# The last three tiles of a decode-attention kernel: a set order, loads in pieces, and the last V rows straight into the result

## Chip, cores, metric

One core of one Trainium2 chip in each set of runs. The metric is device microseconds of one execution. A profile gives, besides, the span from its first to its last instruction, here usually 1.7 to 2 us shorter than the device time.

## The reference, cut to what matters

```
B, H, Sq, Skv, Dh = 8, 32, 1, 4096, 128        # bf16
scores = einsum('bhqd,bhkd->bhqk', q, k) * Dh ** -0.5
attn   = softmax(scores)
out    = einsum('bhqk,bhkd->bhqd', attn, v)
```

There is one query row for each of 256 heads, so every byte of K and V (537 MB together) is used once.

## The kernel before

The heads go in NT = 64 tiles of four heads. K and V of a tile are 4 MB each; a partition holds C = 128 rows of 128 numbers. For each tile:

- `product`: VectorE multiplies K by the query in place (four pieces) and folds 128 columns to 64.
- `sum_over_d`: TensorE adds the 64 columns to 4 with 16 matmuls by the identity (tile `ps`).
- `weights_of`: VectorE adds those four, finds a maximum (`sc`, `pmax`, `spread`, `nmax`, `bias`); ScalarE does four exponentials (`w`).
- `values_of`: 32 matmuls of 512 columns (`av`), four V rows of each partition at a time.
- `result_of`: ScalarE copies `av` to `comb`; four small matmuls with `pick` add the wanted blocks into `op`; after four tiles ScalarE scales `op` by 1/sum and the result is stored.

The parts that the change touches:

```python
    v_cuts = {
        NT - 3: [C // 2] * 2,
        NT - 2: [C // 4] * 4,
        NT - 1: [C // 4] * 3 + [C // 8, C // 8],
    }
    # ... all loads go to one queue, nc.sync, into five 4 MB buffers
    for t in range(NT):
        if t + 2 < NT:
            load("k", t + 2)
        load("v", t)
        # ... q_prep
        product(t, 0, C // 2)
        if t > 0:
            weights_of(t - 1)
        product(t, C // 2, C)
        if t > 1:
            values_of(t - 2, 0, C)
            result_of(t - 2)
            # ... norm_of every fourth tile
        if t < NT - 1:
            sum_over_d(t)
    values_of(NT - 2, 0, C // 2)
    sum_over_d(NT - 1)
    values_of(NT - 2, C // 2, C)
    result_of(NT - 2)
    weights_of(NT - 1)
    norm_of(NQ - 1)
    values_of(NT - 1, 0, C)
    result_of(NT - 1)
```

A scheduler of the framework decides the order on each engine from this; it is not the order of the text. On every engine the instructions then run in that order, so one that waits holds up all behind it (the run with the pieces alone, below, shows two such waits of TensorE, 2.66 and 1.59 us).

## Time and profile before

| | before |
|---|---|
| device time, median of 3 | 1267.79 us (1266.04 to 1267.88) |
| profiled run: time, span | 1269.76, 1267.1 us |
| last V bytes arrive | about 1254 us of the span |
| from there to the end | 13 us |

The page's slices (40 equal ones, 31.7 us each): the busy share of the DMA engines in tenths, and what they moved.

```profile
DMA  9999999999999999999999999999999999999994
GB/s 399 430 430 430 431 432 435 429 431 435 431 430 431 431 430 431 430 433 431 429 430 431 431 434 431 432 429 432 433 432 432 430 431 430 429 429 430 433 425 197
```

Only the first slice and the last two are below the stream's rate. The Trainium skill ("DMA: Bandwidth & Descriptors", Specifications) gives 435 GB/s as the fabric's ceiling, and this trace agrees with 429 to 435 in the other 37. So the body of the kernel cannot go faster without moving fewer bytes. What is left is the end. Here is the chain of waits from 1190 us on: start, duration, and what the end waited for.

```profile
1188.82 36.04 DMA kt<-in_k_dram
...
1224.89 4.49 DVE kt L144 x2
...
1238.25 1.14 DVE kt L147
...
1239.56 1.74 ACT w L197 x8
...
1248.81 2.93 PE ps L161 x13
...
1253.67 1.73 ACT w L197 x8
...
1256.33 7.02 PE av L211 x32
```

The last K lands at 1224.9. Its product, mixed with the weights of tile NT-2, takes VectorE until 1239.4. The last sum (`ps`) is spread between values of NT-2 (the line shows its last 13 matmuls) and ends at 1251.7; only then can the last weights be made, and the last 32 value matmuls start at 1256.3, when all of V has been there for 2 us.

The stretches show what TensorE had to work with: length, busy us of each engine, granted TensorE clock, DMA share, GB/s.

```profile
core 0: us, PE busy (x) PEld busy (x) DVE busy (x) ACT busy (x) POOL busy (x), PEclk, DMA share, GB/s
1237.00:1241.00 4.00, 1.72 (x8) 0.46 (x5) 2.52 (x4) 1.44 (x7) 0.00 (x0) 0.95 1.02 424
1241.00:1245.00 4.00, 3.65 (x12) 1.06 (x12) 0.00 (x0) 0.72 (x3) 0.00 (x0) 0.50 1.01 421
1245.00:1249.00 4.00, 4.00 (x14) 1.01 (x13) 0.00 (x0) 0.00 (x0) 0.00 (x0) 0.70 0.84 345
```

TensorE is idle for more than half of the first stretch, and then gets half its clock for 6.8 us (1240.6 to 1247.4), just when the last sum should go through. The Trainium skill ("TensorE: Matmul & The Clock Gate", Part 1) says that a monitor sets the clock to full or half by windows of about 3.4 us that run freely, not in step with the kernel. The trace agrees: its clock records last 3.41 us or multiples of it and say 1.0 or 0.5.

### The profile page before, as it was taken

The numbers are of one execution on the slowest core, as the hardware profiler recorded it, in microseconds if no ns is written. First come the engines' busy times: TensorE is split into PE (matmuls) and PEld (weight loads), VectorE is DVE, ScalarE is ACT, GpSimd is POOL, SyncE is SP. The second block draws the span as 40 slices with busy tenths as digits, with TensorE's granted clock in tenths as the row PEclk, the third lists the DMA queues.
The fourth block names the chain that finished last, engine by engine and source line by source line (L and its number), as shares of the span: only waits on it lengthen the run. The fifth ranks groups of instructions, "written<-read, shape, count | busy, mean of one in ns | idle before, by whom it ended". The sixth has DMA issues, their size and how long they took to land.

```text
span 1267.1 us, 8759 instructions
## 1 busy us (share of the span) xinstructions
PE 848.8 (67%) x3424; PEld 316.9 (25%) x3424; DVE 939.4 (74%) x850; ACT 164.0 (13%) x609; POOL 2.7 (0%) x13
## 2 busy tenths in 40 slices
PE   1566776766856767658667676676676766757677
PEld 0222222222322222222222222222222222212222
DVE  5869978677687687776877867768678687786771
ACT  0101111111111111101011011110111101101111
POOL 0000000000000000000000000000000000000000
PEclk9778878888879788888787887888877878888888
DMA  9999999999999999999999999999999999999994
GB/s 399 430 430 430 431 432 435 429 431 435 431 430 431 431 430 431 430 433 431 429 430 431 431 434 431 432 429 432 433 432 432 430 431 430 429 429 430 433 425 197
DMA packets 19992, 537.55 MB, mean 424 GB/s; under 512 B 2528, under 2 KB 2528, under 8 KB 2800
## 3 DMA queue, kind: packets, MB, share of 16 engines
q1 hardware_dynamic: 19584, 536.88, 98.7%
q8 instruction: 26, 0.43, 0.1%
q10 hardware_dynamic: 368, 0.13, 0.0%
q14 instruction: 14, 0.11, 0.0%
HBM read 536.94 MB, written 0.07 MB: 424 GB/s over the span
## 4 chain that ended last, share of the span: by engine, by line
DMA 67%; PE 24%; DVE 7%; ACT 1%; issue 0%; DVEq 0%; ACTq 0%
DMA vt<-in_v_dram 63%; PE av L211 22%; DVE kt L144 4%; DMA kt<-in_k_dram 4%; DVE kt L147 2%; PE ps L161 2%; ACT w L197 1%; DVE sc L174 0%; PE op L236 0%; ACT comb L232 0%; DVE pmax L178 0%; DVE bias L189 0%; DVE spread L180 0%; DVE nmax L185 0%; PE zp L222 0%
## 5 line engine op out<-in xcount | busy, mean ns | idle before, releaser
L211 PE MATMUL av<-vt,w 128*16 128x512 bf16 x2048 | 574.8, 450 | 347.4 <-DMA vt<-in_v_dram 345.9
L144 DVE TENSOR_TENSOR kt<-kt,qb 128x4096 bf16<-128x4096 bf16 x256 | 579.3, 2284 | 218.8 <-DMA kt<-in_k_dram 218.7
L211 PEld LDWEIGHTS <-w 128*16 128x16 bf16 x2048 | 207.5, 102 | 711.0 <-issue 541.9
L147 DVE TENSOR_TENSOR kt<-kt 128x2048 bf16<-128x2048 bf16 x256 | 305.9, 1216 | 0.0
L161 PE MATMUL ps<-kt,ident 128*128 128x512 bf16 x1024 | 254.3, 391 | 33.4 <-DVE kt L147 33.4
L197 ACT ACTIVATE w<-sc,bias 128x128 bf16<-128x128 f32 x256 | 110.9, 567 | 749.5 <-DVE bias L189 749.5
L161 PEld LDWEIGHTS <-ident 128*128 128x128 bf16 x1024 | 90.8, 98 | 162.5 <-issue 63.2
L174 DVE TENSOR_REDUCE sc<-ps 128x128 f32<-128x512 f32 x64 | 43.8, 684 | 31.4 <-PE ps L161 31.4
L197 ACT ACTIVATION_READ_ACCUMULATOR w<-sc,bias 128x1 f32 x256 | 64.7, 253 | 0.0
L232 ACT ACTIVATE comb<-av 16x512 bf16<-16x512 f32 x64 | 37.6, 588 | 160.3 <-PE av L211 124.4
L227 DVE RECIPROCAL rz<-zp 16x1 f32<-16x1 f32 x16 | 2.5, 155 | 65.1 <-PE zp L222 65.1
L135 ACT ACTIVATE qb<-qp 128x512 bf16<-128x512 f32 x16 | 9.6, 597 | 178.9 <-DVE kt L144 173.7
L236 PE MATMUL op<-comb,pick 16*16 16x128 bf16 x256 | 25.2, 219 | 5.3 <-ACT comb L232 5.3
L236 PEld LDWEIGHTS <-pick 16*16 16x16 bf16 x256 | 13.8, 85 | 33.0 <-issue 33.0
L129 PE MATMUL qp<-q_all,ident 16*32 16x512 bf16 x64 | 7.6, 430 | 21.3 <-ACT qb L135 14.9
L178 DVE TENSOR_REDUCE pmax<-sc 128x1 f32<-128x128 f32 x64 | 17.8, 279 | 0.1
L180 DVE TENSOR_SCALAR spread<-zero,pmax 128x32 f32<-128x32 f32 x64 | 15.0, 235 | 0.1
L189 DVE TENSOR_SCALAR bias<-own,nmax 128x4 f32<-128x4 f32 x64 | 14.3, 224 | 0.1
L185 DVE TRANSPOSE_TENSOR_REDUCE nmax<-spread 128x1 f32<-128x32 f32 x64 | 13.1, 204 | 0.1
L129 PEld LDWEIGHTS <-ident 16*32 16x32 bf16 x64 | 1.8, 89 | 28.1 <-issue 26.5
L222 PE MATMUL zp<-ones,esum 128*16 128x1 f32 x32 | 3.1, 166 | 8.3 <-ACT w L197 8.3
L245 ACT ACTIVATE stage<-op,rz 16x128 bf16<-16x128 f32 x16 | 5.7, 357 | 10.7 <-PE op L236 10.7
(17 smaller groups left out, 7.6 us busy)
## 6 DMA issues: line engine op xcount, KB each, us to landing
kt<-in_k_dram SPq DMA_DIRECT2D x64, 4096.0 KB, 35.3
vt<-in_v_dram SPq DMA_DIRECT2D x61, 4096.0 KB, 29.6
vt<-in_v_dram SPq DMA_DIRECT2D x7, 1024.0 KB, 28.4
vt<-in_v_dram SPq DMA_DIRECT2D x2, 2048.0 KB, 27.3
vt<-in_v_dram SPq DMA_DIRECT2D x2, 512.0 KB, 17.9
q_all<-in_q_dram ACTq DMA_DIRECT2D x1, 64.0 KB, 5.6
out_dram<-stage ACTq DMA_DIRECT2D x3, 16.0 KB, 10.0
out_dram<-stage ACTq DMA_DIRECT2D x1, 12.0 KB, 8.7
```

The costliest lines, as they stand in the source:

```text
L144: nc.vector.tensor_tensor(out=part, in0=part, in1=qb[:, j : j + 1, :].to_broadcast([P, MC, D]), op=ALU.mult)
L147: nc.vector.tensor_tensor(out=part[:, :, 0 : D // 2], in0=part[:, :, 0 : D // 2], in1=part[:, :, D // 2 : D], op=ALU.add,)
L161: nc.tensor.matmul(ps[:], lhsT=ident[:], rhs=kt[:, u * UC : (u + 1) * UC, s * DS : (s + 1) * DS], start=(s == 0), stop=(s == n - 1),)
L174: nc.vector.tensor_reduce(out=sc[:, u * UC : (u + 1) * UC], in_=ps[:], axis=AX.X, op=ALU.add)
L178: nc.vector.tensor_reduce(out=pmax[:], in_=sc[:], axis=AX.X, op=ALU.max)
L180: nc.vector.tensor_scalar(out=spread[:], in0=zero[:], scalar1=pmax[:, 0:1], scalar2=-scale, op0=ALU.add, op1=ALU.mult,)
L185: nc.vector.tensor_reduce(out=nmax[:], in_=spread[:], axis=AX.X, op=ALU.min, apply_transpose=True)
L189: nc.vector.tensor_scalar(out=bias[:], in0=own[:], scalar1=nmax[:, 0:1], scalar2=None, op0=ALU.add)
L197: nc.scalar.activation(out=w[:, :, g], in_=sc[:], func=ACT.Exp, bias=bias[:, g : g + 1], scale=scale, accum_out=esum[:, t % R, g : g + 1],)
L211: nc.tensor.matmul(avs[t][:], lhsT=w[:, c0 : c0 + CB, :], rhs=vt[:, c0 : c0 + CB, :], start=(c0 == 0), stop=(c0 == C - CB),)
L232: nc.scalar.activation(out=comb[:], in_=avs.pop(t)[:], func=ACT.Copy)
L236: nc.tensor.matmul(ops[n][:], lhsT=pick[:, m, r, :], rhs=comb[:, m * D : (m + 1) * D], start=(r == 0 and m == 0), stop=(r == R - 1 and m = ...
```

## The change

Intent: bring the last product and the last sum forward by halving the last K load and by a hand-set order; cut the V loads finer; and take the last 8 of 128 V rows of each partition out of the block scheme, multiplying them by zero-padded weights straight into `op` (the "direct rows" below), so that they are needed only at the very end.

```diff
+LAST = 8
...
+    w_last = consts.tile([P, LAST, RG], BF16, name="w_last")
+    nc.gpsimd.memset(w_last[:], 0.0)
...
-    v_cuts = {
-        NT - 3: [C // 2] * 2,
-        NT - 2: [C // 4] * 4,
-        NT - 1: [C // 4] * 3 + [C // 8, C // 8],
+    cuts = {
+        ("k", NT - 1): [C // 2] * 2,
+        ("v", NT - 3): [C // 4] * 4,
+        ("v", NT - 2): [C // 4] * 4,
+        ("v", NT - 1): [C // 4] * 3 + [C // 8, C // 16, LAST],
     }
...                                   (in weights_of)
+        if t == NT - 1:
+            nc.vector.tensor_copy(out=w_last[:, :, RG - G : RG], in_=w[:, C - LAST : C, :])
...                                   (in result_of; the stop flags follow)
+        if t == NT - 1:
+            for i in range(LAST):
+                nc.tensor.matmul(
+                    ops[n][:], lhsT=w_last[:, i, :], rhs=loads["v", t][:, C - LAST + i, :],
+                    start=False, stop=(i == LAST - 1),
+                )
...
-    for t in range(NT):
+    for t in range(NT - 1):
...
-        if t < NT - 1:
-            sum_over_d(t)
-    (the end as shown above)
+        sum_over_d(t)
+    load("v", NT - 1)
+    with tc.manual_schedule():
+        product(NT - 1, 0, C // 2)
+        weights_of(NT - 2)
+        product(NT - 1, C // 2, C)
+        values_of(NT - 3, 0, C)
+        result_of(NT - 3)
+        sum_over_d(NT - 1)
+        values_of(NT - 2, 0, C // 2)
+        weights_of(NT - 1)
+        values_of(NT - 2, C // 2, C)
+        result_of(NT - 2)
+        norm_of(NQ - 1)
+        values_of(NT - 1, 0, C - LAST)
+        result_of(NT - 1)
```

More of the change, by code (lines that the diff above doesn't have):

```diff
@@ L116, in load @@
         c0 = 0
-        for n in v_cuts.get(t, [C]) if kind == "v" else [C]:
+        for n in cuts.get((kind, t), [C]):
             nc.sync.dma_start(buf[:, c0 : c0 + n, :], src[t, :, c0 : c0 + n, :])
@@ L212, in values_of @@
                 avs[t][:], lhsT=w[:, c0 : c0 + CB, :], rhs=vt[:, c0 : c0 + CB, :],
-                start=(c0 == 0), stop=(c0 == C - CB),
+                start=(c0 == 0), stop=(c0 + CB == (C if t < NT - 1 else C - LAST)),
             )
@@ L237, in result_of @@
                 ops[n][:], lhsT=pick[:, m, r, :], rhs=comb[:, m * D : (m + 1) * D],
-                start=(r == 0 and m == 0), stop=(r == R - 1 and m == CB - 1),
+                start=(r == 0 and m == 0), stop=(r == R - 1 and m == CB - 1 and t < NT - 1),
             )
+        if t == NT - 1:
[4 more added lines that the diff above has]
+                )
         if r < R - 1:
@@ L270 @@
                 norm_of((t - 2) // R)
-        if t < NT - 1:
-            sum_over_d(t)
-    values_of(NT - 2, 0, C // 2)
-    sum_over_d(NT - 1)
-    values_of(NT - 2, C // 2, C)
-    result_of(NT - 2)
-    weights_of(NT - 1)
-    norm_of(NQ - 1)
-    values_of(NT - 1, 0, C)
-    result_of(NT - 1)
+        sum_over_d(t)
[14 more added lines that the diff above has]
+        result_of(NT - 1)
 _INS = ['q', 'k', 'v']
```

## The prediction

> **What bounds it now.** The page's slices show the DMA engines at 9 tenths and 429 to 435 GB/s in 39 of 40 slices: the body streams K and V (536.9 MB) at the ceiling; each 4 MB tile takes about 9.7 us. The Trainium skill ("DMA: Bandwidth & Descriptors", Specifications) gives a fabric ceiling of 435 GB/s; the trace agrees. The change touches neither bytes nor loop, so only the end can move. Stretches read near the end show traffic thinning from 1247 us and stopping at about 1254 us: the end costs 13 us after the last V bytes.
>
> **Where those 13 us come from** (chain of waits and timeline). The last K lands at 1224.86; its product ends on VectorE at 1239.4, because four product steps (14.5 us) are interleaved with the weights of tile NT-2, which end only at 1241.3. TensorE then mixes the 16 sum-over-d matmuls with values of NT-2, waits for those weights, and runs at granted clock 0.5 from 1240.6 to 1247.4. The sum ends at 1251.7, weights of the last tile at 1255.4, its 32 value matmuls at 1263.3 (all V long landed), and copy, pick, scale and store end at 1267.1.
>
> **After, step by step** (my estimates, from durations of this trace; DMA arrivals kept):
> - First K half lands about 1219.95 (4.9 us before the rest); VectorE is free at 1220.07. Two multiply/add pairs, 6.9 us: 1226.9.
> - VectorE then waits for the sum of NT-2 on TensorE (1228.75), a new wait of about 1.9 us. Five small steps 1.85 us, four exponentials 1.73: weights of NT-2 at 1232.4, 9 us earlier.
> - Second K half's product: 1237.5 (1239.4 before).
> - TensorE takes NT-3's V in quarters (last lands 1234.7), copy 0.6, pick: 1237.6. Tied with VectorE.
> - Sum of NT-1 now undivided: 16 x 0.217 us, ends 1241.3 (was 1251.7: the main gain). Weights of NT-1 at 1245.0 (was 1255.4), hidden under values of NT-2.
> - Values of NT-2 run 1241.1 to 1248.2 with V landed; copy and pick to 1249.4.
> - Values of NT-1, 30 matmuls: to 1256.1. Copy and pick 1257.1; eight 128-wide direct matmuls about 0.6: 1257.7. Scale, store, end: 2.7 us, as before: 1260.4.
>
> So the span drops about 6.7 us, 0.5%. Of that the ordering (weights of NT-2 early, undivided sum, warm clock) earns nearly all. The direct V rows do not: TensorE, not the last V, is then the limit, and eight matmuls replace two of 0.22 us, about +0.2 us. Finer V pieces earn under 1 us. More pieces than eight completion semaphores delay some V issues (NT-2's first waits for a result store that lands at 1215.1), but 8 MB are still queued then, so the stream should not break.
>
> **Clock.** The Trainium skill ("TensorE: Matmul & The Clock Gate", Part 1) says windows of 3.4 us set the clock to full or half. The trace agrees: records last 3.41 or multiples, 1.0 or 0.5. TensorE's idle time after 1220 should now stay below 1.2 us at once, so I expect full clock to the end.
>
> **Predicted time:** 1261.1 us, 8 in 10 between 1259.0 and 1264.0. Chances: faster by 2% 0.005, same 0.985, slower 0.01.
>
> **Right if:** last V lands at 1254 to 1255; granted clock 1.0 from 1220 on; sum of NT-1 in one run of 3.6 us ending near 1241; values of NT-1 begin near 1249.4 without waiting for DMA; the chain of the end is TensorE back to about 1237.
>
> **Wrong if:** a half-clock period falls in 1237 to 1256 (+3.4 us); late issues open a gap in the stream (end moves with it); NT-3's quarters land late; or the direct matmuls cost over 1 us.

## The result

| | before | after |
|---|---|---|
| device time, median of 4 | 1267.84 us (1266.04 to 1268.22) | 1262.40 us (1262.15 to 1262.59) |
| ratio | | 0.996 (0.9943 to 0.9977) |
| span of the profiled run | 1267.1 us | 1260.5 us |

A ratio is the mean time of one kernel's fast runs over that of the other's in the same rounds, so not quite the ratio of the medians. By the 2% rule this is "same", but the interval is clear of 1: 0.4%, 5.4 us by the medians.

The slices of after (31.5 us each):

```profile
DMA  9999999999999999999999999999999999999996
GB/s 400 432 431 431 430 433 430 430 430 430 432 432 430 429 433 432 432 433 431 431 432 433 428 432 432 432 429 430 432 431 430 433 432 432 430 431 431 429 424 287
```

The body is as it was, and no gap opened in the stream. The chain of waits of after (in this kernel L150 and L153 are the product, L167 the sum, L219 the values, L244 the picks, L250 the direct rows):

```profile
1235.01 1.90 PE av L219 x8
...
1237.57 0.38 PE op L244 x4
1237.95 3.57 PE ps L167 x16
1241.51 7.02 PE av L219 x32
...
1249.70 6.51 PE av L219 x30
...
1256.87 0.38 PE op L244 x4
1257.25 0.56 PE op L250 x8
```

From 1235 on the chain lies on TensorE, but for three copies (the lines left out here, 0.59 us each) and the final scale. The sum runs in one piece at full clock and ends at 1241.5 instead of 1251.7; the last values run from 1249.7 to 1256.2 without a wait for V, the last of which lands at 1254.8.

The same stretches in after:

```profile
1237.00:1241.00 4.00, 3.43 (x19) 1.63 (x19) 0.63 (x1) 0.52 (x1) 0.00 (x0) 1.00 1.02 426
1241.00:1245.00 4.00, 4.00 (x20) 1.55 (x19) 1.66 (x5) 1.55 (x8) 0.00 (x0) 1.00 1.00 417
1245.00:1249.00 4.00, 3.52 (x17) 1.34 (x15) 0.18 (x1) 0.64 (x3) 0.00 (x0) 1.00 0.88 359
```

TensorE is busy 10.95 of these 12 us, at full clock. The 4 us from 1241 to 1245 hold 20 matmuls where they held 12.

### The profile page after: what moved, and what is told of

It is laid out like the page before. It is cut to its first block, busy times and chain, and to the rows that moved or that the text cites. A ratio compares the mean times of both kernels' runs of the same rounds, so it can differ in the third digit from the quotient of the medians.

```text
span 1260.5 us, 8779 instructions
## 1 busy us (share of the span) xinstructions
PE 845.2 (67%) x3430; PEld 317.2 (25%) x3430; DVE 940.4 (75%) x851; ACT 164.3 (13%) x609; POOL 2.9 (0%) x14
## 4 chain that ended last, share of the span: by engine, by line
DMA 67%; PE 24%; DVE 7%; ACT 1%; issue 0%; SPq 0%; ACTq 0%; DVEq 0%
DMA vt<-in_v_dram 66%; PE av L219 22%; DVE kt L150 4%; DVE kt L153 2%; PE ps L167 2%; DMA kt<-in_k_dram 1%; ACT w L203 0%; DVE sc L180 0%; PE op L244 0%; ACT comb L240 0%; DVE pmax L184 0%; SPq L124 0%; DVE bias L195 0%; DVE spread L186 0%; DVE nmax L191 0%
## 5 line engine op out<-in xcount | busy, mean ns | idle before, releaser
L219 PE MATMUL av<-vt,w 128*16 128x512 bf16 x2046 | 571.9, 449 | 344.1 <-DMA vt<-in_v_dram 344.1
L150 DVE TENSOR_TENSOR kt<-kt,qb 128x4096 bf16<-128x4096 bf16 x256 | 579.1, 2283 | 214.7 <-DMA kt<-in_k_dram 214.7
L219 PEld LDWEIGHTS <-w 128*16 128x16 bf16 x2046 | 207.6, 102 | 704.3 <-issue 537.3
L153 DVE TENSOR_TENSOR kt<-kt 128x2048 bf16<-128x2048 bf16 x256 | 305.7, 1215 | 0.1
L167 PE MATMUL ps<-kt,ident 128*128 128x512 bf16 x1024 | 253.2, 390 | 32.4 <-DVE kt L153 32.4
L167 PEld LDWEIGHTS <-ident 128*128 128x128 bf16 x1024 | 90.7, 98 | 161.3 <-issue 61.1
L244 PE MATMUL op<-comb,pick 16*16 16x128 bf16 x256 | 25.0, 217 | 6.4 <-ACT comb L240 6.4
L244 PEld LDWEIGHTS <-pick 16*16 16x16 bf16 x256 | 13.7, 84 | 34.2 <-issue 34.2
```

The source lines that it names most:

```text
L150: nc.vector.tensor_tensor(out=part, in0=part, in1=qb[:, j : j + 1, :].to_broadcast([P, MC, D]), op=ALU.mult)
L153: nc.vector.tensor_tensor(out=part[:, :, 0 : D // 2], in0=part[:, :, 0 : D // 2], in1=part[:, :, D // 2 : D], op=ALU.add,)
L167: nc.tensor.matmul(ps[:], lhsT=ident[:], rhs=kt[:, u * UC : (u + 1) * UC, s * DS : (s + 1) * DS], start=(s == 0), stop=(s == n - 1),)
L219: nc.tensor.matmul(avs[t][:], lhsT=w[:, c0 : c0 + CB, :], rhs=vt[:, c0 : c0 + CB, :], start=(c0 == 0), stop=(c0 + CB == (C if t < NT - 1 e ...
L244: nc.tensor.matmul(ops[n][:], lhsT=pick[:, m, r, :], rhs=comb[:, m * D : (m + 1) * D], start=(r == 0 and m == 0), stop=(r == R - 1 and m = ...
```

## The experiments

Every kernel below gave a correct result. "Span" is that of the profiled run, "spans" those of all runs. The kernel before was timed again in each set of runs; its fastest run was 1266.04, 1266.29, 1266.29 and 1266.19 us in the four sets. The record numbers the chips of the last three sets 11, 2 and 13. I take times of different sets to compare to about 0.3 us; a difference of that size needs a trace to back it. The kernel after was timed in the first set only.

### The kernel before once more, unchanged

> Control: the kernel before, unchanged, run as a changed kernel. Ratio 1.000 within 0.1%. Its first profiled run took 1269.8 us with a span of 1267.1, 1.9 us over the median of its runs. Theory: most executions of it have the same stretch at granted clock 0.5 from about 1240.6 to 1247.4 us and a span of 1266 to 1267. Rival: that stretch is an accident of the first profile and is absent here, then the span is about 3 us shorter (near 1263.5).

Measured: 1268.02 us (1266.18 to 1268.79), ratio 0.9988 (0.9975 to 1.0002); span 1264.3, so 2.8 us less than in the first profile, with the same program. Two stretches of it:

```profile
1237.00:1241.00 4.00, 1.72 (x8) 0.46 (x5) 2.53 (x4) 1.44 (x7) 0.00 (x0) 1.00 1.02 426
1241.00:1245.00 4.00, 3.65 (x19) 1.24 (x20) 0.00 (x0) 0.72 (x3) 0.00 (x0) 1.00 1.01 418
```

In the first, TensorE's busy time is the same as in the first profile to 0.01 us, yet the clock stays at 1.0, and the second stretch holds 19 matmuls instead of 12. Over all sets, besides the first profile, the kernel before has 31 runs with a span; they fall into groups: 8 at 1264.3 to 1264.6, 15 at 1265.6 to 1266.4, 7 at 1267.0 to 1267.5, one at 1269.2. A window of 3.41 us at half clock costs about 1.7 us of progress and two cost 3.4, if TensorE is busy throughout, which would make such steps. So the rival here was half right: the first profile showed one of the slower sorts of execution.

### The clock alone: TensorE kept busy in the kernel before

To change nothing else I wrote the scheduler's order of the end out by hand (compared instruction by instruction, it is the same on every engine) and added throw-away matmuls where TensorE waits (shortened, with comments of mine):

```diff
+        warm(5)            # 5 x matmul(keep, lhsT=ident, rhs=kl[:, 0:4, :])
         part_sum(0, 1)     # first matmul of the last sum
+        warm(7)
         vals(NT - 2, 0, 3) # waits for the exponentials of NT-2
```

> The kernel before with its own order of instructions written out by hand (the same on every engine) and twelve throw-away 512-wide matmuls put where TensorE waits before the last sum (5 ahead of its first matmul, 7 after). Theory: the spread of the kernel before (spans 1264.3 to 1269.2 us) is a half-clock stretch that comes or not with the phase of the clock's windows, brought on by TensorE's idle time of 1238.3 to 1241.4 us. Kept busy there, every run has a span near 1264.4, so 1266.1 us with a spread under 0.8 us. Rival: the spread comes from elsewhere; then it stays, 1266 to 1271 us, or the added matmuls only add time.

Measured: 1266.05 us (1265.86 to 1266.43), ratio 0.9987 (0.9975 to 1.0000), spans 1264.1 to 1264.6 in all five runs, while the kernel before beside it had spans of 1264.4 to 1267.4 and times of 1266.29 to 1269.13. Two stretches:

```profile
1237.00:1241.00 4.00, 3.95 (x18) 1.56 (x18) 2.59 (x4) 1.38 (x7) 0.00 (x0) 1.00 0.99 412
1241.00:1245.00 4.00, 3.97 (x20) 1.24 (x19) 0.00 (x0) 0.78 (x3) 0.00 (x0) 1.00 1.02 424
```

With twelve useless matmuls none of the five runs fell into a slower group, where six of the nine beside them did, and they cost nothing against the best group. So the spread of the kernel before is a half-clock stretch that idle time on TensorE brings on in some executions. (Of the slower executions only the first was profiled; that the others are of its kind follows from this run, not from records of theirs.) It is worth about 1.6 us on average (median span of the 31 runs 1265.9, against 1264.3 undisturbed).

### The order alone, and the pieces alone

Order alone (the order of after, with the cuts of before and without direct rows). Against the kernel after, the removal of the direct rows left out:

```diff
-        ("k", NT - 1): [C // 2] * 2,
-        ("v", NT - 3): [C // 4] * 4,
+        ("v", NT - 3): [C // 2] * 2,
-        ("v", NT - 1): [C // 4] * 3 + [C // 8, C // 16, LAST],
+        ("v", NT - 1): [C // 4] * 3 + [C // 8, C // 8],
```

> The kernel before with nothing but the set order of the last tiles; loads cut as before, no direct rows. On record: the ordering earns nearly all of the gain, finer pieces under 1 us, so 1262 to 1263.4 us. Rival: the order needs the pieces. With the last K whole (lands near 1224.9) the last product ends at 1240.5 instead of 1237.6, the sum starts 2.7 us later, so 1265 us; and if TensorE's idle time before it (about 1238.3 to 1240.5) brings back a half-clock stretch, 3.4 us more and the gain is gone, 1266 to 1268 us.

Measured: 1265.57 us (1264.67 to 1266.62), ratio 0.9972; spans 1263.0 to 1263.3 three times (the profiled run among them, at full clock from 1219.4 on) and 1264.8, 1264.9. The prediction fails here: the order alone does not come near 1262.4. From its chain of waits (L163 is the last sum):

```profile
1240.72 3.62 PE ps L163 x16
```

With the last K in one load the product ends at 1240.7, even later than in the kernel before (1239.4), with the weights of NT-2 now whole in front of its second half. The sum starts 2.8 us later than in after.

Pieces and direct rows alone (the cuts of after, the end in the scheduler's order as before):

> The changed kernel's pieces and direct rows with the order left to the scheduler as before. On record: pieces earn under 1 us, so 1266.5 to 1268 us. Rival: the pieces, above all the halved last K, earn most of it: the last product ends near 1234.7, the sum on TensorE ends at about 1241.7, a wait of 1.6 us for the last exponentials comes back, and the end is 2.3 us later than in the changed kernel: 1264 to 1265 us.

Measured: 1266.44 us (1264.45 to 1266.65), ratio 0.9971; spans 1262.7, 1262.9 and three times 1264.7 to 1264.9. The profiled run is of the slower group and has a half-clock record of 3.4 us (1235.1 to 1238.6). Two lines of its timeline, with the idle time before each and what ended it:

```profile
1234.56 2.61 PE L167 MATMUL ps<-kt,ident 128*128 128x512 bf16 x7 [2.66 <-DVE kt L153]
1247.40 0.20 PE L230 MATMUL zp<-ones,esum 128*16 128x1 f32 x2 [1.59 <-ACT w L203]
```

Here the product is done already at 1234.5, but the scheduler put the last sum ahead of a V quarter that lands at 1232.4, and the small matmul `zp`, which needs the last exponentials, ahead of values of NT-2 that need nothing. TensorE waits 2.7 and 1.6 us; for the last 2.1 us of the first wait and the whole of the second there was work that it could have done. So the order is worth its place, and so are the pieces: each alone gives a ratio of 0.997, and it takes both for 0.9945 (next run, same set). By the ratios the two gains just add up (0.28 and 0.29%, together 0.55%).

### Without the direct rows

```diff
-        ("v", NT - 1): [C // 4] * 3 + [C // 8, C // 16, LAST],
+        ("v", NT - 1): [C // 4] * 3 + [C // 8, C // 16, C // 16],
-        values_of(NT - 1, 0, C - LAST)
+        values_of(NT - 1, 0, C)
```

together with the removal of the copy to `w_last` and of the eight matmuls.

> The changed kernel without the direct V rows (32 value matmuls for the last tile, no copy of weights, no eight 128-wide matmuls). Theory as on record: TensorE, not the last V, limits the end, so the direct rows earn nothing: two more matmuls of 0.217 us, eight of 0.07 us less, 0.1 us faster, within 0.3 us of the changed kernel (1262.4). Rival: the direct rows keep the last loads off the tail and are worth 1 us or more, then 1263.4 or over.

Measured: 1262.25 us (1262.10 to 1262.50), ratio 0.9945 in the same set as the two above; span 1260.4 against 1260.5. Its last sum (L164 here) starts when that of after does:

```profile
1237.95 3.57 PE ps L164 x16
```

As predicted, the direct rows earn nothing in this kernel.

### Which piece: K in halves, V in quarters

Both keep the set order and leave out the direct rows. First the order with the halved K only (V as before):

> The order and the halved last K, V cut as before, no direct rows. Theory: the halved K alone brings the last product back to about 1237.6 us, but TensorE must finish V of tile NT-3, of which the second half lands at 1234.8: 16 matmuls to 1238.4, copy and pick to 1239.5, so the sum starts 1.6 us later than in the changed kernel: span 1262.0, 1263.8 us. On record (pieces under 1 us): 1262.4 to 1263.2. If V of NT-3 in quarters is worth nothing: 1262.4.

Measured: 1263.64 us (1263.39 to 1264.46), ratio 0.9969; spans 1261.5 to 1261.9. The sum starts at 1239.3, after the second V half of NT-3 and its copy:

```profile
1239.27 3.57 PE ps L164 x16
```

Then the order with V of NT-3 in quarters only (K whole):

> The order and V of tile NT-3 in quarters, last K whole, no direct rows. Theory: without the halved K the last product ends at 1240.7 us whatever V does, so the quarters are worth nothing here: span about 1263.2, 1265 us as with the order alone (1264.7 to 1266.6). Rival: the quarters are what lets TensorE go on; then about 1263.8 us.

Measured: 1267.19 us (1264.81 to 1267.52), ratio 0.9993 (0.9979 to 1.0006): nothing gained at all. The best of its four spans is 1263.1, that of the order alone; the others are 1264.6 to 1265.8, and the profiled one has half clock from 1241.6 to 1245.0. The product ends at 1240.5, and with the quarters done early TensorE has only more idle time in front of it: 1.10 us busy in the 3.41 us before the drop. The 16 matmuls of the sum take 5.30 us instead of 3.57:

```profile
1240.50 5.30 PE ps L163 x16
```

So the quarters pay only once the halved K has brought the product forward, and then they pay 1.3 us (span 1261.7 to 1260.4 in the kernel without direct rows). That kernel also cuts the last V eighth in two, but its sum already starts 1.3 us earlier (1237.95 against 1239.27), which is the whole difference.

### Inside the order: weights early, sum early

Both undo one line of the changed kernel. Weights of NT-2 behind the whole product:

```diff
         product(NT - 1, 0, C // 2)
-        weights_of(NT - 2)
         product(NT - 1, C // 2, C)
+        weights_of(NT - 2)
```

> The changed kernel with the weights of tile NT-2 moved back behind both halves of the last product. On record: having them early is part of what the ordering earns (they were 9 us earlier), so taking it back should cost some us. Rival: once K is halved they have room: exponentials end at 1237.7, the copy of NT-3 waits 0.7 us for them, sum starts at 1238.65 instead of 1237.9; 0.7 us slower, 1263.1 us.

Measured: 1262.71 us (1262.53 to 1262.84); span 1260.8, 0.3 us over after, no more than sets differ by. But the chain shows where 0.3 us comes from:

```profile
1235.69 1.73 ACT w L203 x8
1237.42 0.43 ACT comb L240
...
1238.27 3.57 PE ps L167 x16
```

The copy of NT-3 waits for the exponentials, and the sum starts 0.32 us later than in after.

The last sum behind the first half of the values of NT-2:

```diff
-        sum_over_d(NT - 1)
         values_of(NT - 2, 0, C // 2)
+        sum_over_d(NT - 1)
         weights_of(NT - 1)
```

> The changed kernel with the last sum over d moved behind the first half of the values of NT-2, so it ends near 1245 us instead of 1241.5. On record: the early, undivided sum is the main gain. If its end is what counts, 3.5 us later, 1266 us. Rival: what counts is that TensorE has no idle time and that the last weights are there before 1249.7; they would come at 1248.9, so nothing is lost but 0.3 us of waiting for V: 1262.6 us.

Measured: 1262.52 us (1262.44 to 1262.53), span 1260.8. From the chain:

```profile
1241.71 3.58 PE ps L167 x16
...
1247.22 1.73 ACT w L203 x8
...
1250.01 6.51 PE av L219 x30
```

The sum ends 3.8 us later than in after, the weights are ready at 1248.95 instead of 1245.2, and the last values start 0.3 us later. So once the pieces and the rest of the order are there, an early sum is worth 0.3 us at most. The reading that fits is that what counts is when TensorE is done with everything that comes before the last values, and it does the same matmuls in either order.

### A version that beats both

If TensorE's work without gaps is what sets the end, its three waits for a copy (0.7 us each in after) and its idle time before the last V quarter of NT-3 are what is left to take. This version splits the last sum by columns of the tile, so that its first half needs only the first half of the product, puts each pick behind the next values, and does the direct rows during the last copy (the four were not tried singly; the bodies of the new helpers are left out):

```diff
-        values_of(NT - 3, 0, C)
-        result_of(NT - 3)
-        sum_over_d(NT - 1)
-        values_of(NT - 2, 0, C // 2)
+        values_of(NT - 3, 0, 3 * C // 4)
+        half_sum(NT - 1, 0)            # 16 matmuls of 256 columns
+        values_of(NT - 3, 3 * C // 4, C)
+        comb_of(NT - 3)                # the copy of result_of
+        half_sum(NT - 1, 1)
+        values_of(NT - 2, 0, C // 4)
+        op_of(NT - 3)                  # the picks of result_of
         weights_of(NT - 1)
-        values_of(NT - 2, C // 2, C)
-        result_of(NT - 2)
+        values_of(NT - 2, C // 4, C)
+        comb_of(NT - 2)
         norm_of(NQ - 1)
-        values_of(NT - 1, 0, C - LAST)
-        result_of(NT - 1)
+        values_of(NT - 1, 0, C // 4)
+        op_of(NT - 2)
+        values_of(NT - 1, C // 4, C - LAST)
+        comb_of(NT - 1)
+        direct(NT - 1)
+        op_of(NT - 1)
+        finish(NT - 1)                 # scale and store
```

> A version meant to beat both: the changed kernel with the last sum in two halves by columns (the first in TensorE's idle time before the last V quarter of NT-3), picks put behind the next values so that no copy is waited for, and the direct rows ahead of the last pick. Theory: TensorE ends its values with the V stream: values of the last tile wait for V again, the last bytes land at 1254.8, span 1259.3, 1261.1 us, 1.2 us under the changed kernel. Rival: TensorE's busy time is what counts and 32 half-width matmuls cost more than 16: no gain, 1262.4 or over.

Measured: 1261.02 us (1260.97 to 1261.04), ratio 0.9947 to its set's kernel before; spans 1259.2 to 1259.3. From its timeline:

```profile
1249.81 1.89 PE L231 MATMUL av<-vt,w 128*16 128x512 bf16 x8 [0.22 <-DMA vt<-in_v_dram]
1252.28 3.18 PE L231 MATMUL av<-vt,w 128*16 128x512 bf16 x14 [0.58 <-DMA vt<-in_v_dram]
1255.30 0.61 PE L257 MATMUL op<-vt,w_last 128*16 128x128 bf16 x8
```

TensorE waits for V again, so the stream is the limit nearly to the end. The same without the direct rows:

> The tight version without the direct rows: all 32 value matmuls for the last tile. In the changed kernel they were worth nothing, because TensorE was behind the V stream. Theory: in the tight version V is the limit, so they now pay: without them the last two matmuls (0.45 us) come ahead of the copy, 0.5 us slower, 1261.5 us. Rival: worth nothing here either, 1261.0.

Measured: 1261.23 us (1261.08 to 1261.36), spans 1259.4 to 1259.6. By the medians the direct rows are worth 0.2 us here, not the 0.5 us expected; the two runs are from different sets, so this alone would not show it. The last copy, first with the direct rows and then without:

```profile
1255.50 0.59 ACT comb L253
```

```profile
1255.79 0.59 ACT comb L251
```

That is 0.29 us in their favour. The run without them had its third V quarter 0.14 us earlier (1252.10 against 1252.24); with equal arrivals the difference would be 0.43 us by this count, about the two value matmuls saved.

## Why the prediction was right, and where it was wrong

**The span was right, and step by step.** Predicted 1260.4, measured 1260.5; the steps (last product 1237.5, sum end 1241.3, last values 1256.1, direct rows 1257.7) were each within 0.3 us of the trace. No late issue opened a gap. What failed is what was added to that sum: the subtraction from a median, and the shares given to its parts.

**The time was 1.3 us too low: 1261.1 against 1262.4, inside the range.** The step is "So the span drops about 6.7 us" taken off the median of 1267.8. The drop was counted from a profile with a span of 1267.1, one of the slower clock groups; its run took 1269.8 us, not 1267.8. The median of the kernel before goes with a span of about 1265.9 (31 runs), so the term was 5.4 us. Adding the usual 1.85 us to the predicted span would have given 1262.3.

**"The ordering (weights of NT-2 early, undivided sum, warm clock) earns nearly all" was wrong.** Counting by the spans of executions without a half-clock record near the end (each kernel has such a profile): before 1264.3; order alone 1263.0 to 1263.3; order and halved K 1261.7; with V finer too 1260.4; with direct rows 1260.5. So of 3.8 us, added in this order, the set order earned about 1.2, the halved K about 1.5, the finer V about 1.3. The shares depend on the order of adding: the pieces alone have 1262.7 and 1262.9 in their two fastest runs (not profiled, taken to be at full clock), and with the set order put on top of them last, it earns about 2.3. Neither is nearly all. The chain of after was predicted with the pieces in it, and then credited to the order. Taken back singly, early weights and an early sum are worth at most 0.3 us each, which is at the limit of what sets can show and rests on the chains.

**"Finer V pieces earn under 1 us" was too low, and incomplete:** 1.3 us behind a halved K, nothing without it (shown within the set order).

**Clock.** Right that it stays full from 1220 to the end of after. Missed: in the kernel before the half-clock stretch comes only in some executions. Keeping TensorE busy there gives about 1.6 us on average, shown by the throw-away matmuls; 3.8 and 1.6 make up the 5.4 us. It also explains the spreads: 0.4 us in after, over 2 us in before.

**Direct rows.** Right: worth nothing while TensorE is behind V (1262.25 without, 1262.40 with).

**Open.** Where exactly the limit lies below which the monitor drops the clock: the traces bracket it (last section), but windows with 1.41 to 1.69 us busy went either way, and the ends of matmuls in a trace are modelled. And some executions, most of them of the kernel before, took 2.3 to 3.7 us more than their span instead of about 1.85; no run here says why.

## What to carry to other kernels

When a stream bounds the body, look for the engine that runs without a gap from the last loads to the end, and lay its queue so that no instruction that must wait stands before one that need not; in these runs a piece of a load was worth something where it fed that engine earlier, and of two inputs of one join, cutting the earlier one (V) paid only when the later one (K) had been brought forward too. Take the profile of one execution as one draw: before subtracting its time from a median, see whether its clock records are those of a typical run. A gain that was added up as one chain must not be shared out among its parts by feeling; each part needs its own run, alone and taken back.

## What the Trainium skill lacked or had wrong

- "TensorE: Matmul & The Clock Gate", Part 1: its table of the two states has the clock fall "after ≥1 idle window (~3.4µs)". Here a window need not be idle. Windows (the 3.41 us before a drop) with TensorE busy 1.52, 1.10 and 0.76 us were followed by half clock, in the kernel before, with V in quarters only, and with the pieces alone; one with 2.31 us busy, in the second profile of the kernel before, was not:

```profile
1237.20:1240.61 3.41, 1.52 (x7) 0.37 (x4) 2.33 (x4) 1.05 (x5) 0.00 (x0) 1.00 1.01 423
```

```profile
1236.18:1239.59 3.41, 2.31 (x12) 0.81 (x9) 3.35 (x4) 0.03 (x1) 0.00 (x0) 1.00 1.02 423
```

  The page gives no share at which a window counts as idle; the clock records of the 13 traces bracket one, but for a few matmul records that a trace can miss. (The clock also drops some 60 times in each run's body, where TensorE waits for V.) All 774 drops after the first 20 us followed a window with TensorE busy 0 to 1.69 us, and the 2429 full-clock windows that kept the clock had it busy 1.41 to 3.41 us. So in this case the clock fell below about 1.4 us busy of 3.41 (41%) always, and above 1.7 (50%) never.
- The same page, in the same part, puts the cost of its warm-up ramp under 1% of a typical span and says that the number of slow matmuls varies from run to run. The stretches at the end here agree in size (spans 1264.3 to 1269.2 us for one program, 0.4%), but the page lacks that this spread is nearly as large as the whole gain from tuning a kernel's end (5.4 us), and that a few throw-away matmuls in an idle gap took it away (1264.1 to 1264.6).
- "DMA: Bandwidth & Descriptors" (Why a DMA increments its semaphore by 16 and not by 1) says that a DMA's engines finish independently; no page says by how much they drift apart on one long queue. The DMA share falls over about 7 us at the end of before (0.84 in 1245 to 1249, 0.47 in 1249 to 1253), so the last piece arrives long after the stream begins to thin. No view tells the engines apart, but the traces fit a drift: in after, by the landing times in its trace, the V quarters go on landing every 2.4 to 2.5 us up to 1252.3, while the GB/s fall with the share (417 at 1.00, 359 at 0.88, 200 at 0.50), as if some engines had run out of work and the latest kept its pace.
